# Retention and a gated feed-forward on one core: attention scores as quarter products, and an earlier release of one pair's loads

## The chip, the cores and the metric

The kernel runs on one core of a Trainium2 chip. The core has a matrix engine (TensorE, PE in the profile, with its weight loads as PEld), a vector engine (VectorE, DVE), an activation engine (ScalarE, ACT), GpSimd (POOL), and SyncE (SP), which here issues transfers. Sixteen DMA engines move data. The metric is the device time of one execution in microseconds (us).

## The reference

Retention over four batches and eight heads, 768 steps, 64 elements a head, and then a feed-forward layer with a sigmoid gate on all 3,072 tokens:

```python
gamma = 1 - 2 ** (-5 - arange(H)); scale = 1 / sqrt(D)
for t in range(S):
    state = gamma * state + einsum('bhd,bhe->bhde', k[:, :, t], v[:, :, t])
    y[:, :, t] = scale * einsum('bhd,bhde->bhe', q[:, :, t], state)
x = y.transpose(0, 2, 1, 3).reshape(B * S, H * D)
out = (sigmoid(x @ w_gate) * (x @ w_val)) @ w_out
```

Sizes: x is 3072 x 512, w_gate and w_val 512 x 1536, w_out 1536 x 512. Inputs and output are 32-bit; the kernel multiplies in bf16.

## The kernel before, in words

The 768 steps are cut into six chunks of 128. Two batches of one chunk form a *pair*, so there are 12 pairs, 0 to 11; pair i is chunk i // 2, and within it j = 0, 1 names the batch. The eight heads lie as four columns p of two heads e = 0, 1, and head e occupies partitions 0 to 63 or 64 to 127 (`half(e)`). For the second batch the two heads of a column are swapped.

The work on a pair is written as small functions, each of which issues for its own engines:

- `load_kq`, `load_v` (lines 53 to 72): seven transfers a pair, issued by POOL, which also turn 32-bit into bf16.
- `xbar` (L213): two transposing transfers, issued by SP, k first and then q, into the tile `kqX`. Pair 2 is transposed on TensorE instead (L207).
- `scale_k` (L218): POOL weighs k for the state.
- `inter` (L242): the old state times q, 16 products that use 64 rows and 64 columns of TensorE's array each.
- `scores` (L226): k times q inside the chunk, 16 products of 64 rows and 128 columns, the two heads of a column on the two halves of the rows. They go into four PSUM banks, one for each batch and head.
- `mask` (L232): DVE weighs the scores and writes bf16.
- `intra` (L249): masked scores times v, 16 products of 128 rows and 64 columns, added to what inter left.
- `y_out` (L265): DVE scales the sum into `xT`, the input of the feed-forward.
- `state` (L272), `state_sum` (L281), `casts` (L285): k times v, the running state in 32-bit, and its bf16 copy for a later inter.

`block(old, new)` puts these in TensorE's order: inter of the old pair, scores of the new one, intra of the old one, state of the new one. Either pair may be missing. The steps with both are those of old 4, 5, 6, 7, 8, 9, 10 with new 5 to 11; pairs 3 and 4 have their scores in a step without an old pair, and pair 2 has its own in the middle of the first feed-forward.

The feed-forward runs on a chunk of all four batches, 512 tokens: `up` (L364, L382, L383) for gate and value, `down` (L399, L403) for the output. The order of everything is written out by hand. Pairs 0 and 1 and the first chunk's feed-forward come first; afterwards the list `plan` names, for each chunk, after which group of up or down a step is issued. The tile framework adds the semaphores. Every engine runs its own instructions in the order in which they were issued.

POOL is kept back at seven places by `hold` (L496), a copy of one element of `kqX` into the tile `held`. The copy can start only when the transfer that writes that element has landed, and the load issues behind it on POOL wait with it. The first one stands between `scale_k(3)` and the loads of pairs 4 and 5 (lines 514 to 518). The indices of `kqX` are partition (head and element), k or q, batch, column and token.

PSUM has eight banks, which all parts take in turn from one pool (`pf`, `bank`).

Of the kernel before, what the change touches and what calls it, by code (L numbers as in the profile page):

```python
# [15 lines left out]
def kernel(  # L16
# [12 lines left out]
    nc = tc.nc  # L29
# [3 lines left out]
    C = 128  # L33
    NT = S // C
    NP = H // 2
# [14 lines left out]
    kn, qn, ks, vs, kqT = {}, {}, {}, {}, {}  # L50
# [138 lines left out]
    xT, sc, stA, stB, y, za, zz, zb = {}, {}, {}, {}, {}, {}, {}, {}  # L189

    def bank(shape, dt=F32):
        return pf.tile(shape, dt, tag="ff", name="ff")

    def half(e):
        return slice(e * D, (e + 1) * D)
# [20 lines left out]
    def scale_k(i):  # L216
        ks[i] = ld.tile([C, 2 * H, D], BF16, tag="ks", name="ks", bufs=3)
        nc.gpsimd.tensor_tensor(ks[i], kn[i], tabsk[:, i // 2].rearrange("s j h -> s (j h)").unsqueeze(2)  # L218
                                .to_broadcast([C, 2 * H, D]), op=ALU.mult)

    def scores(i, j):
        t = kqT[i]
        sc[i, j] = (bank([128, NP, C]), bank([128, NP, C]))
        for p in range(NP):
            for e in range(2):
                nc.tensor.matmul(sc[i, j][e][:, p, :], t[half(e), 0, j, p, :], t[half(e), 1, j, p, :],  # L226
                                 start=True, stop=True)

    def mask(i, j, e):
        st = stB if e else stA  # L230
        st[i, j] = at.tile([128, NP, C], BF16, tag=f"st{e}", name=f"st{e}", bufs=4)
        nc.vector.tensor_tensor(st[i, j], sc[i, j][e], maskk[:, e ^ j], op=ALU.mult)  # L232

    def new_y(i):
        for j in range(2):
            y[i, j] = bank([128, NP, C])

    def inter(i):
        for p in range(NP):
            for j in range(2):  # L240
                for e in range(2):
                    nc.tensor.matmul(y[i, j][half(e ^ j), p, :], zb[i - 2][half(e), j, p, :],  # L242
                                     kqT[i][half(e), 1, j, p, :], start=(p == 0), stop=False, skip_group_check=True)

    def intra(i, j):
        for p in range(NP):
            for e in range(2):
                st = (stA, stB)[e ^ j][i, j]
                nc.tensor.matmul(y[i, j][half(e), p, :], vs[i][:, j * H + 2 * p + e, :], st[:, p, :],  # L249
                                 start=False, stop=True, skip_group_check=True)  # L250
# [9 lines left out]
    def y_out(i, j):  # L260
        t = i // 2
        if t not in xT:
            new_xT(t)
        c = (i % 2 * 2 + j) * C
        nc.vector.tensor_tensor(xT[t][0][:, :, c:c + C], y[i, j], taby, op=ALU.mult)  # L265

    def state(i):
        zz[i] = bank([128, 2, NP, D])
        for j in range(2):
            for p in range(NP):  # L270
                for e in range(2):
                    nc.tensor.matmul(zz[i][half(e), j, p, :], ks[i][:, j * H + 2 * p + e, :],  # L272
                                     vs[i][:, j * H + 2 * p + (e ^ j), :],
                                     start=(j == 0 and p == 0), stop=True, skip_group_check=True)
# [4 lines left out]
    def state_sum(i):  # L279
        new_za(i)  # L280
        nc.vector.tensor_tensor(za[i], za[i - 2], zz[i], op=ALU.add)  # L281
# [5 lines left out]
    def block(old, new):  # L287
        last = new is None or new >= NPAIR - 2
        if old is not None:
            new_y(old)  # L290
            inter(old)
        for j in range(2):
            if new is not None:
                scores(new, j)
        for j in range(2):
            if old is not None:
                intra(old, j)
        if not last:
            state(new)
        for j in range(2):  # L300
            if old is not None:
                y_out(old, j)
        for j in range(2):
            if new is not None:
                mask(new, j, 0)
                mask(new, j, 1)
        if not last:
            state_sum(new)
# [180 lines left out]
    def load_next(i):  # L489
        load_kq(i)  # L490
        load_v(i)

    held = const.tile([128, 1], BF16, name="held")

    def hold(i):
        nc.gpsimd.tensor_copy(held, kqT[i][:, 1, 1, NP - 1, C - 1:C])  # L496

    load_next(3)
    scale_k(2)
# [6 lines left out]
    for b in range(3):  # L506
        down(0, b, 6, 9)
    for j in range(2):
        scores(2, j)
        mask(2, j, 0)  # L510
        mask(2, j, 1)
    for b in range(3):
        down(0, b, 9, 12)
    xbar(3)
    scale_k(3)
    hold(3)
    load_next(4)
    load_next(5)
    down(0, 3, 0, 6)
# [4 lines left out]
    for j in range(2):  # L524
# [7 lines left out]

    plan = {
        1: [(2, block, None, 3), (4, block, 3, None), (4, xbar, 4), (4, scale_k, 4), (4, hold, 4), (4, load_next, 6),
            (5, casts, 3), (7, xbar, 5), (7, scale_k, 5), (11, block, None, 4), (12, casts, 4), (12, xbar, 6), (12, scale_k, 6),
            (12, hold, 6), (12, load_next, 7), (14, block, 4, 5), (16, casts, 5), (18, block, 5, 6), (19, casts, 6)],
        2: [(0, xbar, 7), (0, scale_k, 7), (0, hold, 7), (0, load_next, 8), (8, block, 6, 7), (10, casts, 7), (10, xbar, 8),
            (10, scale_k, 8), (10, hold, 8), (10, load_next, 9), (17, block, 7, 8), (19, casts, 8)],
# [47 lines left out]
```

## Time and profile before

| what | value |
|---|---|
| median of 5 runs | 227.84 us (227.26 to 228.27) |
| the profiled execution, its own time | 227.63 us |
| its span, first to last instruction | 225.8 us |
| TensorE busy | 220.4 us (98%) |
| DVE, POOL, ACT busy | 113.4, 106.0, 70.3 us |
| share of the ending chain: up (L364), down (L399) | 54%, 27% |
| the same: scores (L226), inter (L242), intra (L249), state (L272) | 3%, 2%, 3%, 1% |

"Busy" counts an engine's instructions without pauses between them. The chain that ended last is followed back from the last instruction, each time to what released it or to the instruction before it on its engine; its shares say where a saving would reach the end. A line such as L226 is a line of the kernel. Matmul ends are modelled, their starts are recorded, so distances below are taken from start to start.

### The profile page before, as it was taken

The numbers are of one execution on the slowest core, as the hardware profiler recorded it, in microseconds if no ns is written. First come the engines' busy times: TensorE is split into PE (matmuls) and PEld (weight loads), VectorE is DVE, ScalarE is ACT, GpSimd is POOL, SyncE is SP. The second block draws the span as 40 slices with busy tenths as digits, with TensorE's granted clock in tenths as the row PEclk, the third lists the DMA queues.
The fourth block names the chain that finished last, engine by engine and source line by source line (L and its number), as shares of the span: only waits on it lengthen the run. The fifth ranks groups of instructions, "written<-read, shape, count | busy, mean of one in ns | idle before, by whom it ended". The sixth has DMA issues, their size and how long they took to land.

```text
span 225.8 us, 4323 instructions
## 1 busy us (share of the span) xinstructions
PE 220.4 (98%) x1758; PEld 116.9 (52%) x1758; DVE 113.4 (50%) x199; ACT 70.3 (31%) x121; POOL 106.0 (47%) x128
## 2 busy tenths in 40 slices
PE   7899999999999999999999999999999999999994
PEld 2644444558888555445445445445445444444444
DVE  7753653064963996845806535905434802333301
ACT  7584232334233112332222332321432321333221
POOL 8999998845996919359391090730000000000000
PEclk9999999999999999999999999999999999999999
DMA  9999999997999999989999699792600012100022
GB/s 128 153 171 195 191 193 176 168 240 137 116 162 144 154 204 124 140 86 129 85 142 140 139 74 153 56 129 107 139 0 0 3 46 93 49 1 0 0 93 96
DMA packets 105780, 25.72 MB, mean 114 GB/s; under 512 B 94752, under 2 KB 102816, under 8 KB 105760
## 3 DMA queue, kind: packets, MB, share of 16 engines
q0 software_dynamic: 80928, 13.90, 80.2%
q1 hardware_dynamic: 23648, 11.21, 23.5%
q10 hardware_dynamic: 1184, 0.33, 0.6%
q8 instruction: 14, 0.23, 0.4%
q14 instruction: 6, 0.05, 0.1%
HBM read 28.31 MB, written 6.29 MB: 153 GB/s over the span
## 4 chain that ended last, share of the span: by engine, by line
PE 97%; DVE 1%; ACT 1%; issue 0%
PE ff L364 54%; PE ff L399 27%; PE ff L226 3%; PE ff L426 3%; PE ff L249 3%; PE ff L373 2%; PE ff L242 2%; PE ff L412 1%; PE ff L272 1%; ACT kqT L320 1%; PE ff L319 1%; DVE st L326 1%; PE ff L336 0%; PE ff L207 0%; PE ff L350 0%
## 5 line engine op out<-in xcount | busy, mean ns | idle before, releaser
L383 DVE TENSOR_TENSOR hT<-gs,ff 128x512 bf16<-128x512 f32 x72 | 49.0, 686 | 61.2 <-PE ff L364 57.8
L364 PE MATMUL ff<-xT,wg 128*128 128x512 bf16 (+1 forms) x328 | 71.7, 348 | 0.0
L364 PE MATMUL ff<-xT,wv 128*128 128x512 bf16 (+1 forms) x328 | 71.7, 348 | 0.0
L382 ACT ACTIVATE gs<-ff 128x512 f32<-128x512 f32 x72 | 42.9, 597 | 84.1 <-PE ff L364 81.6
L399 PE MATMUL ff<-wo,hT 128*128 128x512 bf16 x276 | 62.1, 379 | 0.0
L364 PEld LDWEIGHTS <-wv 128*128 128x128 bf16 x328 | 32.1, 98 | 28.4
L364 PEld LDWEIGHTS <-wg 128*128 128x128 bf16 x328 | 31.5, 98 | 27.8
L399 PEld LDWEIGHTS <-hT 128*128 128x128 bf16 x276 | 26.3, 98 | 30.7
L403 ACT COPY ob<-ff 128x512 f32<-128x512 f32 x23 | 13.5, 586 | 58.6 <-PE ff L399 58.5
L232 DVE TENSOR_TENSOR st<-ff,maskk 128x512 bf16<-128x512 f32 x40 | 24.7, 680 | 6.4 <-PE ff L226 6.4
L265 DVE TENSOR_TENSOR xT<-ff,taby 128x512 bf16<-128x512 f32 x20 | 12.9, 685 | 28.9 <-PE ff L249 28.9
L496 POOL COPY held<-kqX 128x1 bf16<-128x1 bf16 x7 | 1.8, 259 | 38.0 <-DMA kqX<-qn 38.0
L218 POOL TENSOR_TENSOR ks<-kn,tabsk 128x1024 bf16<-128x1024 bf16 x8 | 15.6, 1959 | 0.4 <-PE ff L399 0.4
L67 POOL DMA_DIRECT2D qn<-in_q_dram x20 | 15.4, 796 | 0.0
L67 POOL DMA_DIRECT2D kn<-in_k_dram x20 | 15.2, 770 | 0.0
L57 POOL DMA_DIRECT2D vs<-in_v_dram x10 | 12.1, 1206 | 1.1 <-DMA wo<-in_moe_w_out_dram 1.0
L285 DVE TENSOR_TENSOR zb<-za,tabz 128x512 bf16<-128x512 f32 x10 | 10.3, 1033 | 0.2
L63 POOL DMA_DIRECT2D kn<-in_k_dram x10 | 9.3, 929 | 1.5 <-issue 1.5
L426 PE MATMUL ff<-zero 128*128 128x512 bf16 x22 | 8.4, 507 | 1.2 <-DVE zero L135 1.2
L63 POOL DMA_DIRECT2D qn<-in_q_dram x10 | 9.2, 921 | 0.0
L249 PE MATMUL ff<-st,vs 128*64 128x128 bf16 x160 | 6.4, 222 | 0.0
L79 POOL DMA_DIRECT2D wg<-in_moe_w_gate_dram x7 | 5.8, 838 | 0.0
(73 smaller groups left out, 118.6 us busy)
## 6 DMA issues: line engine op xcount, KB each, us to landing
out_dram<-ob SPq DMA_DIRECT2D x23, 256.0 KB, 2.6
vs<-in_v_dram POOLq DMA_DIRECT2D x10, 256.0 KB, 6.5
kn<-in_k_dram POOLq DMA_DIRECT2D x13, 128.0 KB, 4.7
qn<-in_q_dram POOLq DMA_DIRECT2D x13, 128.0 KB, 4.6
wo<-in_moe_w_out_dram POOLq DMA_DIRECT2D x4, 384.0 KB, 6.6
wg<-in_moe_w_gate_dram POOLq DMA_DIRECT2D x5, 256.0 KB, 6.1
wv<-in_moe_w_val_dram POOLq DMA_DIRECT2D x5, 256.0 KB, 6.6
kn<-in_k_dram POOLq DMA_DIRECT2D x20, 64.0 KB, 3.6
```

The costliest lines, as they stand in the source:

```text
L63: nc.gpsimd.dma_start(out=tiles[i][:, 0:H], in_=src[0])
L67: nc.gpsimd.dma_start(out=dst[:, e], in_=pairs[:, 1 - e])
L218: nc.gpsimd.tensor_tensor(ks[i], kn[i], tabsk[:, i // 2].rearrange("s j h -> s (j h)").unsqueeze(2) .to_broadcast([C, 2 * H, D]), op=ALU.mult)
L232: nc.vector.tensor_tensor(st[i, j], sc[i, j][e], maskk[:, e ^ j], op=ALU.mult)
L249: nc.tensor.matmul(y[i, j][half(e), p, :], vs[i][:, j * H + 2 * p + e, :], st[:, p, :], start=False, stop=True, skip_group_check=True)
L265: nc.vector.tensor_tensor(xT[t][0][:, :, c:c + C], y[i, j], taby, op=ALU.mult)
L364: nc.tensor.matmul(u[:, i * n:(i + 1) * n], w[:, kk, n1 * 128:(n1 + 1) * 128], x_of(t, kk, lo, hi), start=(kk == 0), stop=(kk == KT - 1))
L382: nc.scalar.activation(g, ps[0], AX.Sigmoid)
L383: nc.vector.tensor_tensor(hT[t][:, n1s[0]:n1s[-1] + 1, lo:hi], g.rearrange("p (i n) -> p i n", n=n), ps[1].rearrange("p (i n) -> p i n", n ...
L399: nc.tensor.matmul(o, hT[t][:, n1, b * C:(b + 1) * C], wo[:, n1, :], start=(n1 == 0), stop=(n1 == NFF - 1))
L403: nc.scalar.copy(ob, o)
L426: nc.tensor.matmul(u, zero[:, :128], zero, start=True, stop=True)
```

## The change

Two things. A new function `quarter_scores` issues the scores as products of 64 rows and 64 columns: each former product is cut in two by the columns of k (g = 0, 1), which gives 32 products a pair, and the output goes to the same banks, half of the partitions at a time. `block` uses it in place of `scores`, and so does pair 2; pairs 0 and 1 keep `scores`. And `hold` takes an argument that chooses k or q; the first hold, that of pair 3, now names k (0), all the others stay at q (1).

```diff
+    def quarter_scores(i, j):
+
+        t = kqT[i]
+        sc[i, j] = (bank([128, NP, C]), bank([128, NP, C]))
+        for p in range(NP):
+            for g in range(2):
+                for e in range(2):
+                    nc.tensor.matmul(sc[i, j][e][half(g), p, :], t[half(e), 0, j, p, half(g)], t[half(e), 1, j, p, :],
+                                     start=True, stop=True)
+
...
         for j in range(2):
             if new is not None:
-                scores(new, j)
+                quarter_scores(new, j)
...
-    def hold(i):
-        nc.gpsimd.tensor_copy(held, kqT[i][:, 1, 1, NP - 1, C - 1:C])
+    def hold(i, which=1):
+        nc.gpsimd.tensor_copy(held, kqT[i][:, which, 1, NP - 1, C - 1:C])
...
     for j in range(2):
-        scores(2, j)
+        quarter_scores(2, j)
         mask(2, j, 0)
         mask(2, j, 1)
...
-    hold(3)
+    hold(3, 0)
     load_next(4)
     load_next(5)
```

## The prediction, made before the result was known

> **What bounds the kernel now.** I read the page first, for the engine that carries the end and for its clock:
>
> ```profile
> span 225.8 us, 4323 instructions
> PE 220.4 (98%) x1758; PEld 116.9 (52%) x1758; DVE 113.4 (50%) x199; ACT 70.3 (31%) x121; POOL 106.0 (47%) x128
> ...
> PEclk9999999999999999999999999999999999999999
> ...
> PE 97%; DVE 1%; ACT 1%; issue 0%
> ```
>
> TensorE is 97% of the chain that ended last, and its granted clock is full in all 40 slices. The list of waits shows no matmul waiting for another engine once the first two pairs are through. So time is saved only by a shorter run of matmuls, and is lost if one has to wait. Next I read TensorE's timeline around the step for old pair 8 and new pair 9, around the first step of pair 3 (scores, then state) and around the last step (pair 11: inter, then intra):
>
> ```profile
> 103.63 0.59 PE L364 MATMUL ff<-xT,wv 128*128 128x512 bf16 x2
> 104.15 0.42 PE L242 MATMUL ff<-kqX,zb 64*64 64x128 bf16 x16
> 104.50 0.62 PE L226 MATMUL ff<-kqX 64*128 64x128 bf16 x16
> 105.05 0.64 PE L249 MATMUL ff<-st,vs 128*64 128x128 bf16 x16
> 105.52 0.42 PE L272 MATMUL ff<-vs,ks 128*64 128x64 bf16 x16
> ```
> ```profile
> 55.80 0.62 PE L226 MATMUL ff<-kqX 64*128 64x128 bf16 x16
> 56.35 0.44 PE L272 MATMUL ff<-vs,ks 128*64 128x64 bf16 x16
> ```
> ```profile
> 187.89 0.42 PE L242 MATMUL ff<-kqX,zb 64*64 64x128 bf16 x16
> 188.23 0.64 PE L249 MATMUL ff<-st,vs 128*64 128x128 bf16 x16
> ```
>
> The first column is the start, the second the length, and "64*128" the part of the array that a matmul uses. The reader is to see how long one kind lasts until the next begins: 0.35 us for inter, 0.55 for scores, 0.47 for intra. A merged row ends with its last matmul, so its length less one matmul gives the spread of its starts. The rows by line give one matmul:
>
> ```profile
> L226 PE MATMUL ff<-kqX x144: 216/216/227, 55.8 to 174.1; 64*128 64x128 bf16 x144
> ```
> ```profile
> L242 PE MATMUL ff<-kqX,zb x144: 216/216/240, 60.3 to 188.1; 64*64 64x128 bf16 x144
> ```
>
> Inter: 0.42 - 0.216 = 0.20 us for 16 starts. In the trace's single starts these are four groups of four, 3 to 4 ns apart inside a group; the second group comes 0.08 after the first, the others every 0.056. Scores: 0.62 - 0.216 = 0.40 us for eight groups of two, the second after 0.066, the others every 0.056. So four quarter products take the time of two half products.
>
> From the start of the last group to the next kind it is 0.15 to 0.16 us wherever the part of the array changes (inter to scores, scores to intra, scores to state, and inter to intra at 188.23). Where it does not change there is no such gap: intra to state, both "128*64", go on after 0.053 (105.05 + 0.64 - 0.219 = 105.47, and state starts at 105.52). A change of shape thus costs about 0.10 us more than an ordinary group.
>
> **The change, part by part.**
>
> Scores as quarters. Per pair, 16 half products go and 32 quarter products come, in eight groups of four instead of eight groups of two. The running rate is not shown for 32 quarters in a row; nearest are the 16 of inter, 0.056 per group, the same interval as now. Upper bound: only two of four run at once (scores' own pairs: two per 0.056), then +0.45 us per pair. Lower bound: state's two-wide groups, which stream half as many columns, start every 0.028; but the present groups of 128 columns all take 0.053 to 0.056, so I exclude a gain. I take 0.056, as inter has this very shape, these four places and two banks for the two row halves.
>
> Inter to scores. In seven steps (new pairs 5 to 11) scores follow inter directly. Bounds: 0.056, as if one kind went on (0.053 at intra to state), or 0.15 as today. I take 0.056, since the shape is then the same. From inter's start to intra's start now: 105.05 - 104.15 = 0.90. Then: twelve groups, 0.08 + 10 x 0.056 = 0.64, and the way out to intra 0.156 as for pair 11 (188.23 - 187.89 - 0.19), together 0.796. That is -0.104 each, -0.73 for seven.
>
> Pairs 2, 3 and 4 follow full-array matmuls. Entry 0.31 before and after (inter after such a matmul has it: 103.63 + 0.59 - 0.379 = 103.84 to 104.15), first group 0.08 in place of 0.066, exit 0.156 in place of 0.149: 0.08 + 6 x 0.056 + 0.156 = 0.57 instead of 0.55. +0.02 each, +0.06 for three.
>
> Weight loads: 32 instead of 16 per pair, 106 ns instead of 94 each, beside matmuls (inter's are hidden today). Uncovered, 8 x 12 ns = 0.1 us a pair.
>
> The masks read the same four banks, a tenth of a microsecond earlier in the seven steps. DVE moves with TensorE there: at 105.51 it had been idle for 0.49 us, so output and masks shift along.
>
> The earlier release on POOL. The copy that holds POOL waits for the crossbar of pair 3's k instead of q. Views of the issues and of the copy:
>
> ```profile
> L213 SPq DMA_TRANSPOSE kqX<-kn x1: 1492/1492/1492, 47.9 to 47.9; - x1
> L213 SPq DMA_TRANSPOSE kqX<-qn x1: 1850/1850/1850, 49.5 to 49.5; - x1
> ```
> ```profile
> 53.50:54.00 0.50, 0.50 (x7) 0.45 (x6) 0.00 (x0) 0.39 (x1) 0.44 (x2) 1.00 0.13 45
> 54.00:54.50 0.50, 0.50 (x7) 0.45 (x5) 0.27 (x1) 0.00 (x0) 0.50 (x1) 1.00 0.00 0
> 54.50:55.00 0.50, 0.50 (x7) 0.45 (x5) 0.42 (x1) 0.00 (x0) 0.50 (x2) 1.00 0.00 0
> ```
>
> By its time to landing k lands at 47.88 + 4.74 = 52.62, q at 49.49 + 3.95 = 53.43 (the copy started at 53.49). So the 14 transfer issues of pairs 4 and 5 behind it on POOL, the scaling of k for pair 4 (65.5 us), and on SP the crossbars of pair 4, which wait for those loads, come up to 0.81 us earlier. The windows (last two columns DMA share and GB/s) show nothing moving from 54.0 to 55.0 after the first issue at 53.73: packets come 1.5 us behind it. Released at 52.7 they would start near 54.4, and q has landed a microsecond before. So q of pair 3, needed at 55.80, keeps its 2.4 us. Worth on the path: 0, because pair 4's q lands at 69.26 (62.41 + 6.86) for scores at 73.64 and pair 5's at 76.70 for scores at 78.84. Bounds: a gain is excluded, no matmul waits for either; if the loads did catch q, the longest landing of the crossbar (7.3 us) puts it at 56.8, a stall of 1.0 us.
>
> Sum: -0.73 + 0.06 + 0 = -0.67 us. The profiled execution took 227.63 us (span 225.8 and 1.8 around it), so 226.96; the median of the runs is 0.21 above it, so **227.17**, or -0.29%.
>
> **A cost that the trace only bounds: feeding TensorE.** Inter, scores, intra and state make 64 pairs of load and matmul today, 80 then. Two sequencer rows show how quickly pairs are handed over:
>
> ```profile
> L226 PEldq EVENT_SEMAPHORE  x1: 51/51/51, 104.2 to 104.2; - x1
> ```
> ```profile
> L272 PEldq EVENT_SEMAPHORE  x1: 51/51/51, 105.1 to 105.1; - x1
> ```
>
> The first stands ahead of scores, the second ahead of state. Between them 16 scores and 16 intra pairs, 64 instructions, were handed over in 0.9 - 0.05 = 0.85 us: at most 13.3 ns each, 26.6 a pair. The quarters use 14 a pair (0.056 / 4). Both events come about 20 ns after the start of the kind before them (104.15, 105.05), and so does state's event of pair 3 (55.8, scores start 55.80), where the sequencer had 2 us. So it was waiting for room, not behind. I take it as fast enough; the bound goes to the rivals.
>
> The Trainium skill, Runtime: NRT & Kernel Launch, section "Instruction fetch mechanics", names a floor of about 20 sequencer cycles for an instruction; TensorE: Matmul & The Clock Gate, section "Wait — 56ns, not 53.3ns?", gives that sequencer 1.2 GHz. An estimate from the two pages is 33 ns a pair, which would put seven steps late by 0.4 to 0.7 us each and the run near 232. The 64 instructions in 0.85 us are already quicker than that floor, so the measurement decides.
>
> **Rivals.**
> 1. The sequencer limits (slower). Place: the 32 quarters after inter, handed over from 104.25 on. At 26.6 ns a pair the last starts at 105.10 instead of 104.79; state's last, 64 pairs and one event later, at 106.0, today 105.75. +0.25 in five steps with state, +0.2 in two without: +1.65 + 0.06, so 229.5. It cancels the gain from about 22 ns a pair on. For it: no stretch of 48 quarters exists today. Against: the 20 ns above.
> 2. The shape still changes, or is charged anyway, between inter and scores: ten times +0.02, 228.0. Against: intra to state.
> 3. Two wide only: 10 x 0.45, near 232.
> 4. A late crossbar, or POOL's earlier scaling blocking DVE at a worse moment: up to +1.0, 228.2. Against: the spare times above.
> 5. A better way out of the quarters, or a wait unseen by me removed: 226.8.
>
> **How the numbers follow.** As computed 64%, 226.9 to 227.5 by the spread of the runs (227.26 to 228.27 before); rival 1 13%, rival 2 8%, rivals 3 and 4 4% each, rival 5 7%. A measurement of this kernel tells about 0.3%, 0.68 us, from no change: the limit is 227.16, in the middle of the computed case, which I split 35 to 29. Faster 0.35 + 0.07 = 0.42; same 0.29 + 0.08 + 0.03 (a mild rival 1) = 0.40; slower 0.10 + 0.04 + 0.04 = 0.18. The range 226.7 to 228.2 holds the computed case and rivals 2, 4 and 5, and leaves out most of rivals 1 and 3.
>
> **What would show it.** Right: 32 scores matmuls "64*64" in a pair; scores' first start 0.25 after inter's first instead of 0.35; inter to intra 0.80 instead of 0.90; pairs 3 and 4 at 0.57; POOL's first copy near 52.7; no matmul waiting. Wrong: groups of four more than 0.056 apart, above all late among the 32 (rival 1); 0.35 still there (rival 2); scores of pair 3 waiting for q (rival 4).

## The result, and the profile after

The changed kernel takes 226.81 us in the median of 27 runs (226.52 to 227.91); the kernel before took 227.75 us in the median of 51 (227.2 to 229.41). The ratio is 0.9958, with a 95% interval of 0.9947 to 0.9969: faster by 0.94 us in the medians, 0.42%. The forecast was 227.17 us, -0.67 us, in a range of 226.7 to 228.2.

The page of the changed kernel:

```profile
span 224.7 us, 4643 instructions
PE 219.4 (98%) x1918; PEld 116.2 (52%) x1918; DVE 113.1 (50%) x199; ACT 70.4 (31%) x121; POOL 105.5 (47%) x128
```

There are 160 more matmuls, and TensorE's busy time and the span are both smaller. Its timeline around the same three steps (start, length, engine, line, operation; scores are L236 now, inter L252, intra L259, state L282):

```profile
103.68 0.42 PE L252 MATMUL ff<-kqX,zb 64*64 64x128 bf16 x16
103.92 0.62 PE L236 MATMUL ff<-kqX 64*64 64x128 bf16 x32
104.47 0.64 PE L259 MATMUL ff<-st,vs 128*64 128x128 bf16 x16
104.94 0.42 PE L282 MATMUL ff<-vs,ks 128*64 128x64 bf16 x16
```
```profile
55.50 0.64 PE L236 MATMUL ff<-kqX 64*64 64x128 bf16 x32
56.07 0.44 PE L282 MATMUL ff<-vs,ks 128*64 128x64 bf16 x16
```
```profile
186.88 0.42 PE L252 MATMUL ff<-kqX,zb 64*64 64x128 bf16 x16
187.23 0.64 PE L259 MATMUL ff<-st,vs 128*64 128x128 bf16 x16
```

Scores now begin 0.24 us after inter (0.35 before), inter to intra is 0.79 us (0.90 before, 0.796 forecast), and a pair's scores without an inter ahead take 0.57 us (0.55 before, 0.57 forecast). Pair 11, where nothing was changed, still has 0.35. From the first matmul of the first feed-forward, which starts at 15.29 us (15.61 before), to the first down after pair 11's intra, at 187.80 (188.80 before), it is 172.51 us against 173.19: -0.68, the sum of the forecast to 0.01 us. The rest of the difference between the two spans (225.8 and 224.7) is the earlier start, -0.32, which varies from execution to execution (15.29 to 15.62 us in the profiles of this study), and some 0.05 at the end. Two further profiles of the changed kernel show 172.60 and 172.72 us for the same stretch; in both the difference stands at 18.8 us, where the first feed-forward waited 0.09 and 0.21 us for weights.

The copy that holds POOL, and the crossbar transfers of pair 3 (durations in ns, and behind the comma the first and the last start in us):

```profile
L506 POOL COPY held<-kqX x1: 191/191/191, 52.9 to 52.9; 128x1 bf16<-128x1 bf16 x1
```
```profile
L213 SPq DMA_TRANSPOSE kqX<-kn x1: 2062/2062/2062, 47.6 to 47.6; - x1
L213 SPq DMA_TRANSPOSE kqX<-qn x1: 1947/1947/1947, 49.8 to 49.8; - x1
```

The copy runs at 52.9 instead of 53.49, though the transfers themselves landed a little later here (k at 52.86, q at 53.76). In these two profiles no matmul waits for anything after the first pairs, so they show no use for the release. The medians, however, moved 0.27 us more than the sum, and the upper end of the runs came down: 18 of the 51 runs before were above 228.0, 0.8 us over the lowest, and 5 of the 27 after are as far above theirs. That was the question for the experiments.

### The profile page after: what moved, and what is told of

It is laid out like the page before. It is cut to its first block, busy times and chain, and to the rows that moved or that the text cites. A ratio compares the mean times of both kernels' runs of the same rounds, so it can differ in the third digit from the quotient of the medians.

```text
span 224.7 us, 4643 instructions
## 1 busy us (share of the span) xinstructions
PE 219.4 (98%) x1918; PEld 116.2 (52%) x1918; DVE 113.1 (50%) x199; ACT 70.4 (31%) x121; POOL 105.5 (47%) x128
## 4 chain that ended last, share of the span: by engine, by line
PE 93%; POOL 2%; DMA 2%; issue 0%; DVE 0%; POOLq 0%
PE ff L374 54%; PE ff L409 27%; PE ff L259 3%; DMA vs<-in_v_dram 2%; PE ff L236 2%; PE ff L383 2%; PE ff L252 2%; POOL kn L92 1%; PE ff L422 1%; POOL qn L92 1%; PE ff L282 1%; PE ff L436 1%; PE ff L346 1%; PE ff L207 0%; PE ff L360 0%
## 5 line engine op out<-in xcount | busy, mean ns | idle before, releaser
L506 POOL COPY held<-kqX 128x1 bf16<-128x1 bf16 x7 | 1.3, 186 | 39.3 <-DMA kqX<-qn 34.5
L259 PE MATMUL ff<-st,vs 128*64 128x128 bf16 x160 | 6.4, 222 | 0.0
L336 DVE TENSOR_TENSOR st<-ff,decay 128x512 bf16<-128x512 f32 x8 | 5.2, 686 | 1.5 <-PE ff L226 0.9
```

## The experiments

Two theories stood against each other: A, the shape change between inter and scores is the whole gain and the release is worth nothing; B, the release gave a part. Medians are compared with the kernel before in the same group of runs, on the same chip; the ratios are formed over all the runs of a group and need not equal the quotient of the medians.

**The two parts, one at a time.** The quarters alone, run twice:

```diff
-    hold(3, 0)
+    hold(3)
```

> The changed kernel with its first hold back at pair 3's q, so the quarter products alone. Theory A (the whole gain is the shape change that is gone between inter and scores in seven steps, -0.73, less 0.06 for the slower entry of pairs 2, 3 and 4; the release is worth nothing): median 0.67 below the kernel before, ratio 0.997, and the same as the changed kernel within 0.1 us. Theory B (the runs of the changed kernel moved by 0.94 us in their median, 0.27 more than that sum, and the earlier release gave the rest): ratio 0.997 too, but the changed kernel run beside it is 0.27 us quicker than this one. In the profile both expect 0.25 us from inter's first start to scores' first start and first loads of pair 4 about 0.8 us later than in the changed kernel.

> The quarter products alone once more, beside the changed kernel. Theory A (the release is worth nothing; the 0.65 us between the two medians, 227.30 and 226.65, was scatter): both medians equal within 0.15 us. Theory B2 (without the release some executions have pair 5's scores wait for the crossbar of its q, as in the profile of the one-batch run, where it landed at 78.72 us): this one 0.3 to 0.6 us above the changed kernel, with most of its runs between 226.6 and 227.7.

The release alone, run twice, is the changed kernel with `scores` put back at both places:

```diff
-                quarter_scores(new, j)
+                scores(new, j)
...
-        quarter_scores(2, j)
+        scores(2, j)
```

> Scores as half products everywhere, as before, and only the first hold moved to pair 3's k. Theory A: no matmul waits for these loads, so ratio 1.000 (within 0.1 us of the kernel before). Theory B: 0.27 us below the kernel before, ratio 0.9988. Both expect the copy on POOL near 52.7 to 53 us instead of 53.5, and inter to scores still 0.35 us.

> Half products as before and only the first hold moved to pair 3's k, once more. Theory B2 (the release spares waits of some executions around pair 5: scores for its q, state for its scaled k, down for a bank that the output of pair 4 frees late): 0.1 to 0.5 us below the kernel before in the median, depending on how many of that kernel's runs wait, with fewer runs above 228. Theory D (the release matters only together with the quarters): equal to the kernel before within 0.1.

And the changed kernel itself, beside the first and the second of the quarters alone:

> The changed kernel again, beside the others on one chip. Theory A: 0.67 below the kernel before (0.9971), equal to the quarters alone. Theory B: 0.94 below (0.9958), which is the sum of the two parts.

> The changed kernel once more. Both theories: 226.5 to 226.9, ratio 0.995 to 0.997. Its pair 5 q should land near 77.2 us, a microsecond ahead of the scores that read it at 78.5.

| kernel | median us | before, same group | ratio, 95% interval |
|---|---|---|---|
| quarters alone, first | 227.30 | 227.55 | 0.998 (0.9961 to 0.9999) |
| release alone, first | 227.71 | 227.55 | 1.0003 (0.9982 to 1.0024) |
| changed kernel, with the first | 226.65 | 227.55 | 0.995 (0.9931 to 0.997) |
| quarters alone, second | 227.96 | 228.05 | 0.9992 (0.9972 to 1.0012) |
| changed kernel, with the second | 226.84 | 228.05 | 0.9947 (0.9927 to 0.9968) |
| release alone, second | 227.65 | 227.89 | 0.9982 (0.9963 to 1.0002) |

Theory A fails for the release: with the quarters in place it is worth 0.65 us in the first group (227.30 to 226.65) and 1.12 in the second (227.96 to 226.84). The runs of the quarters alone go from 226.58 to 228.87, and in the second group half of them lie above 228, as do half of the runs of the kernel before (12 of 24); of the 13 runs of the changed kernel beside them none is above 227.24. Theory A holds for the rest: the profile of the quarters alone has the same steps as the changed kernel,

```profile
104.02 0.42 PE L252 MATMUL ff<-kqX,zb 64*64 64x128 bf16 x16
104.27 0.62 PE L236 MATMUL ff<-kqX 64*64 64x128 bf16 x32
104.81 0.58 PE L259 MATMUL ff<-st,vs 128*64 128x128 bf16 x14
```

so its 0.7 us are there, and in many runs something takes them back. A little of that is in the two profiles themselves, both of quick runs (226.83 and 227.13 us). In the first, state of pair 5 starts 0.66 us after intra instead of 0.47, because it waits for POOL's scaled k:

```profile
79.15 0.64 PE L259 MATMUL ff<-st,vs 128*64 128x128 bf16 x16
79.81 0.44 PE L282 MATMUL ff<-vs,ks 128*64 128x64 bf16 x16
```

In the second, down waits 0.31 us at 81.8 for an output of pair 4. From the first feed-forward to the first down after pair 11 they take 172.72 and 172.82 us; without these waits that is 172.53 and 172.51, as in the changed kernel. In neither do pair 5's scores wait for q. The release alone is unclear in both groups: +0.16 and -0.24 in the medians, with intervals that contain 1.

**Half of the scores as quarters.** From the kernel before, with `quarter_scores` added:

```diff
-                scores(new, j)
+                (quarter_scores if j == 0 and old is not None else scores)(new, j)
```

> In the seven steps that have an inter, only the first batch's scores are quarter products and the second batch's stay half products; pairs 2 to 4 and the hold are as before. The shape then still changes once between inter and intra's shape, only one batch later. Theory A: no gain, inter's start to intra's start 0.90 us as before, ratio 1.000; the gap of 0.15 us stands between the two batches. Theory C (quarter products are quicker in themselves, whatever stands before them): half of the gain, inter to intra 0.85, -0.36 us, ratio 0.9984.

Median 227.51 against 227.55, ratio 0.9997 (0.9982 to 1.0013). Its timeline:

```profile
104.29 0.42 PE L252 MATMUL ff<-kqX,zb 64*64 64x128 bf16 x16
104.54 0.39 PE L236 MATMUL ff<-kqX 64*64 64x128 bf16 x16
104.87 0.40 PE L226 MATMUL ff<-kqX 64*128 64x128 bf16 x8
105.19 0.64 PE L259 MATMUL ff<-st,vs 128*64 128x128 bf16 x16
```

Inter to intra is 0.90 us as before: the quarters follow inter after 0.25 us, and the 0.1 us is paid a little later, between the quarters and the half products (0.33 for four groups that need 0.22). Quarter products are not quicker in themselves; what they save is the change of shape. Theory C falls.

The same profile also held the first direct sight of the other effect. The chain that ended last, around pair 5's scores (start, us, what):

```profile
49.45 4.83 DMA kqX<-qn
54.33 0.19 POOL held L506
...
64.47 6.83 DMA qn<-in_q_dram
71.44 7.28 DMA kqX<-qn
78.72 0.14 issue
78.85 0.42 PE ff L236 x16
```

In this execution q of pair 3 landed at 54.3 instead of 53.4, the loads behind the hold came a microsecond later, pair 5's q was loaded at 71.3, and its crossbar landed at 78.72. Inter of pair 4 had started at 78.24, its scores could have followed at 78.49 and waited 0.37 us. In the profile before, the same transfer had landed at 76.70 with 2.1 us to spare.

**The suspected wait made larger.** The quarters alone, with two operations on POOL behind the first hold:

```diff
     hold(3)
+    late = const.tile([128, NP, C], F32, name="late")
+    for _ in range(2):
+        nc.gpsimd.tensor_tensor(late, causal.unsqueeze(1).to_broadcast([128, NP, C]),
+                                tabsk[:, 0, 0, 0::2].unsqueeze(2).to_broadcast([128, NP, C]), op=ALU.mult)
```

> The quarter products alone, with two more operations of about 1.07 us each on POOL behind the first hold (they write a tile that nobody reads), so that the loads of pairs 4 and 5 start some 2.1 us later. Theory A, with the spare 2.1 us between landing and use of the profile before: no more than 0.1 to 0.2 us above the quarters alone. Theory B2, with a spare between 0 and 3 us from execution to execution: pair 5's scores wait in most runs, 0.7 to 2 us above the quarters alone, and the gap stands between inter of pair 4 and scores of pair 5.

Median 231.0 against 228.05 of the kernel before, ratio 1.0124 (1.0092 to 1.0155): 3.0 us above the quarters alone of the same group, more than the delay put in. The timeline (in brackets the idle time ahead and what ended it):

```profile
78.42 0.42 PE L252 MATMUL ff<-kqX,zb 64*64 64x128 bf16 x16
82.00 0.64 PE L236 MATMUL ff<-kqX 64*64 64x128 bf16 x32 [3.17 <-DMA kqX<-qn]
82.57 0.64 PE L259 MATMUL ff<-st,vs 128*64 128x128 bf16 x16
83.05 0.42 PE L282 MATMUL ff<-vs,ks 128*64 128x64 bf16 x16
83.79 6.64 PE L409 MATMUL ff<-wo,hT 128*128 128x512 bf16 x23 [0.33 <-issue]
```

Pair 5's scores waited 3.3 us for its q, and from state to the next inter (at 90.36) it took 7.3 us instead of 5.6 in the changed kernel (79.49 to 85.12). What lengthened the second stretch is the granted clock of TensorE, the third column from the end in these windows:

```profile
83.00:84.00 1.00, 0.67 (x25) 0.62 (x21) 0.97 (x2) 0.00 (x0) 0.00 (x0) 0.72 2.02 166
84.00:85.00 1.00, 1.00 (x3) 0.29 (x2) 1.00 (x3) 0.00 (x0) 0.00 (x0) 0.50 1.28 237
85.00:86.00 1.00, 1.00 (x4) 0.37 (x3) 1.00 (x2) 0.00 (x0) 0.00 (x0) 0.50 1.26 328
86.00:87.00 1.00, 1.00 (x4) 0.36 (x3) 1.00 (x3) 0.59 (x1) 0.36 (x2) 0.57 0.39 150
```

After 3.2 us without a matmul the clock stood at about half for more than 3 us; the four windows lack 1.7 us of clock in all, which is the 7.3 against 5.6. So the wait was paid for once and a half. Five of the six runs have a mean clock of 0.992 or 0.993 in this kernel, and the sixth, at 0.999, is the quickest (230.02). A wait of 1.4 us in another profile below left the clock at 1.00. Theory A's spare of 2.1 us does not hold in this kernel, where loads that were issued 2.4 us later than in the quarters alone left q 3.2 us late, and what stands behind the first hold reaches the path.

**The hold taken away.**

```diff
-    hold(3, 0)
     load_next(4)
     load_next(5)
```

> The changed kernel without its first hold: the loads of pairs 4 and 5 are issued about 5 us earlier, near 48, beside the crossbars of pair 3. Theory A: pair 4's and 5's crossbars land earlier for nothing; if the loads slow pair 3's crossbars past 55.4 us, where its scores start, the run is longer by the overshoot (landing at most 9.5 us after its issue at 49.7: up to 3.8 us). Theory B2: pair 5's q lands several microseconds ahead of 78.5, so no wait there, and the median is at or under the changed kernel's unless pair 3 is late in the same way.

Median 228.34 against 228.05, ratio 1.0019 (0.9995 to 1.0044), and 1.5 us above the changed kernel. Pair 3's scores come 6.33 us after the up before them began, 5.33 in the changed kernel, and start at 57.00:

```profile
55.04 1.04 PE L374 MATMUL ff<-xT,wv 128*128 128x256 bf16 x8
57.00 0.64 PE L236 MATMUL ff<-kqX 64*64 64x128 bf16 x32 [0.93 <-DVE hT L393]
```
```profile
L213 SPq DMA_TRANSPOSE kqX<-qn x1: 1870/1870/1870, 50.4 to 50.4; - x1
...
DMA to landing us min/median/max: 6.5/6.5/6.6
```

The bracket names DVE, which had been done for long; q was issued at 50.41 and took 6.45 us to land, at 56.86, against 4.0 us in the changed kernel, and scores started 0.14 us behind it. So loads beside pair 3's crossbars do slow them, by 2.4 us here, and cost a wait of 1.0 us. This is the fourth rival of the prediction, in a kernel that provokes it. The release to k stays on the good side: nothing moves between 54.0 and 54.5 in the changed kernel's windows, and q had landed at 53.76, before the first of the new loads' packets.

**Which wait is it?** In the profile of the second release alone, the slowest of its twelve runs, it was another one. DVE there:

```profile
77.56 3.89 DVE L295 TENSOR_TENSOR zb<-za,tabz 128x512 bf16<-128x512 f32 x1
81.37 1.27 DVE L275 TENSOR_TENSOR xT<-ff,taby 128x512 bf16<-128x512 f32 x2
```
```profile
77.05 3.84 POOL L218 TENSOR_TENSOR ks<-kn,tabsk 128x1024 bf16<-128x1024 bf16 x2
```
```profile
80.31 1.47 PE L409 MATMUL ff<-wo,hT 128*128 128x512 bf16 x6
82.10 2.10 PE L409 MATMUL ff<-wo,hT 128*128 128x512 bf16 x9 [0.33 <-DVE xT L275]
```

The bf16 copy of pair 4's state, 0.69 us long where POOL is quiet, lasted 3.89 us and ended 0.56 us after POOL's two scalings of k. The Trainium skill, SBUF — State Buffer, section "SBUF: two separate sides", has DVE and GpSimd share a pair of ports that one holds for a whole instruction while the other blocks, where the DVE operation has two inputs in SBUF and GpSimd's reads SBUF too; that is so here, and the copy that outlasts both scalings agrees with it. Pair 4's output stood behind the copy, and down waited 0.5 us for the output. POOL's scalings come behind its loads, so a later release moves this wait as well. To see whether it is the main one, the quarters alone with that copy issued behind the step of pairs 4 and 5:

```diff
-(12, casts, 4), (12, xbar, 6)
+(12, xbar, 6)
...
-(14, block, 4, 5), (16, casts, 5)
+(14, block, 4, 5), (15, casts, 4), (16, casts, 5)
```

> The quarter products alone, first hold at q, with the bf16 copy of pair 4's state issued behind the step of pairs 4 and 5. If what the release spares is mainly the wait of down behind that copy (DVE holds it while POOL scales k, 3.62 us in the profile of the quarters alone, and the output of pair 4 starts only at 81.1), the median comes down to that of the changed kernel, 226.7 to 226.9, ratio 0.995 to 0.997. If it is mainly pair 5's scores waiting for q, nothing is gained: ratio 0.998 to 0.999 as for the quarters alone.

Median 227.96 against 227.89, ratio 1.0005 (0.9979 to 1.0032): nothing gained. Its profile has no long copy any more, but

```profile
78.43 0.42 PE L252 MATMUL ff<-kqX,zb 64*64 64x128 bf16 x16
80.22 0.64 PE L236 MATMUL ff<-kqX 64*64 64x128 bf16 x32 [1.37 <-DMA kqX<-qn]
```

pair 5's scores waited 1.5 us for q, which landed at 80.08. So the copy behind POOL is not what the release mainly spares; the crossbar of pair 5's q is the likelier one. That it is the main wait of the quarters alone is not shown: of its runs only two quick ones have a profile, and there q came in time.

The kept profiles show why q comes close at all. The third column is the time from the first load of pair 4 behind the hold to the landing of pair 5's last load of q, the fourth how far ahead of its scores the crossbar of that q landed (us, one figure for each profile):

| kernel | first hold | first load to q loaded | spare of the crossbar |
|---|---|---|---|
| before | q | 16.1 | 2.1 |
| release alone | k | 16.3, 17.3 | 3.1, 2.4 |
| one batch as quarters (pairs 2 to 4 half products) | q | 16.7 | -0.2 |
| quarters alone | q | 18.9, 18.5 | 0.3, 1.1 |
| quarters with the late copy | q | 19.1 | -1.4 |
| changed kernel | k | 18.5, 18.4, 19.2 | 1.2, 1.5, 0.9 |

Wherever pairs 2 to 4 have quarter products, these loads take about 2 us longer (18.3 and 18.4 in the kernels with later loads and with smaller products, 16.5 in the version below, which goes back to half products there), and most of the spare time of the kernel before is gone; the release gives 0.8 us back. With one batch as quarters the loads are quick, but they began 0.8 us late, and the crossbar itself took 7.3 us. Why the loads take longer is not shown. One thing that differs in the traces is a 16 KB transfer of instructions: it starts at 68.7 to 70.2 us in the lower three kernels, while the loads are in flight, and at 71.2 to 72.1 us in the upper three, behind them. No run tests whether it matters.

**A version made from this.** The changed kernel with half products again for pairs 2, 3 and 4, and the late copy:

```diff
-                quarter_scores(new, j)
+                (scores if old is None else quarter_scores)(new, j)
...
-        quarter_scores(2, j)
+        scores(2, j)
...
-(12, casts, 4), (12, xbar, 6)
+(12, xbar, 6)
...
-(14, block, 4, 5), (16, casts, 5)
+(14, block, 4, 5), (15, casts, 4), (16, casts, 5)
```

> The changed kernel with half products again for pairs 2, 3 and 4, and with the bf16 copy of pair 4's state issued three groups later, behind the step of pairs 4 and 5, so that the output of pair 4 does not stand behind it on DVE. Expected: pairs 2 to 4 back at 0.55 us for their scores, 0.06 us less in all; output of pair 4 on DVE near 79.9 instead of 80.5; median 0.05 to 0.1 below the changed kernel, 226.5 to 226.7, ratio 0.994 to 0.996.

226.92 against 227.89, ratio 0.9961 (0.9936 to 0.9986), which is not told apart from the changed kernel and not the 0.05 to 0.1 us below it that were expected. Pairs 2 to 4 are back at 0.55 us. Seven of its twelve runs are under 227.0; the profiled one, 227.61, has no wait around pair 5 but lost 0.9 us between 18 and 20 us, where the first feed-forward waited for its weights.

**Smaller products still.** Each quarter product cut into two of 64 moving columns:

```diff
+            for m in range(2):
...
-                    nc.tensor.matmul(sc[i, j][e][half(g), p, :], t[half(e), 0, j, p, half(g)], t[half(e), 1, j, p, :],
-                                     start=True, stop=True)
+                        nc.tensor.matmul(sc[i, j][e][half(g), p, half(m)], t[half(e), 0, j, p, half(g)],
+                                         t[half(e), 1, j, p, half(m)], start=True, stop=True)
```

> The changed kernel with each quarter product cut once more, into two of 64 moving columns: 64 scores products a pair, the same array work. Theory of a sequencer with room to spare: state's groups of 64 columns start every 28 ns, so 16 groups of four take 0.45 us as now, inter to intra 0.80, the same time. Theory of a limit on handing over (at most 26.6 ns a pair of load and matmul was shown, 14 in the quarters): a group of four then lasts longer than 28 ns; at 14 ns a pair scores take 0.90 instead of 0.45, +4.5 us over ten pairs.

```profile
105.22 0.42 PE L253 MATMUL ff<-kqX,zb 64*64 64x128 bf16 x16
105.46 0.71 PE L237 MATMUL ff<-kqX 64*64 64x64 bf16 x64
106.11 0.64 PE L260 MATMUL ff<-st,vs 128*64 128x128 bf16 x16
```

Median 228.29 against 227.89, ratio 1.0011 (0.9987 to 1.0034). Scores to intra is 0.65 us instead of 0.55, so ten pairs cost 1.0 us more, and inter to intra is 0.89, nearly as with the half products. The single starts of the 64 products have two parts: the first half comes in groups of four, 32 ns apart, and from then on one product starts every 8.3 ns without groups. Pair 3's, which follow a long stretch of full-array products, keep to groups of four almost to the end. A group of four every 32 ns is 8.0 ns a product, so the rate itself hardly changes.

## Why the prediction was right, and where it was not

**Scores as quarters, 0.056 us per group:** right. 32 quarters run in eight groups of four at 0.056, as inter's 16 do; the upper bound of two at a time did not occur.

**Inter to scores at 0.056 instead of 0.15:** right. The step is 0.79 us, 0.796 forecast; the kernel with one batch as quarters shows that the 0.10 us belong to the change of shape, since they come back where the shape changes one batch later.

**Pairs 2, 3 and 4, +0.02 each:** right, 0.57 us.

**Weight loads hidden:** right. The row of single loads gives 103 to 107 ns, and no group is longer for it.

**The release, "Worth on the path: 0", with the words "a gain is excluded":** this is the step that failed. The spare times of 4.4 us for pair 4 and 2.1 us for pair 5 were read from one execution of the kernel before and taken to hold for the changed kernel. With the quarters and the same hold, the spare of pair 5's q is 0.3 and 1.1 us in two profiles of quick runs and less than nothing in the one with the late copy. The chain is hold, loads of pairs 4 and 5, crossbar of pair 5's q, scores of pair 5, and beside it POOL's scaling of k with the waits behind that; 0.8 us earlier at its head is worth 0.65 and 1.12 us in the medians with the quarters in place. It is by this term that the measured -0.94 exceeds the -0.67. The forecast still came within 0.4 us because the term is small, and for that it gave no reason. And without it the other term would hardly have shown: the quarters alone came to -0.25 and -0.09.

**No collision of the earlier loads with q:** right for this release; without the hold q is slowed from 4.0 to 6.45 us and pair 3 waits 1.0 us.

**The feeding of TensorE, bound at 26.6 ns a pair of load and matmul, 14 needed, taken as fast enough:** right, and with room to spare. With 64 products the starts settle at 8.3 ns each, so handing over takes no more than that. The 33 ns estimated from the Trainium skill (Runtime: NRT & Kernel Launch, "Instruction fetch mechanics") is four times too slow here; its floor for an instruction does not bind weight loads and matmuls in these runs.

What stays open. The table of spare times fits what the parts do: the release alone has nothing to shorten where q is 2 to 3 us early, the quarters alone use that time up, and both together leave 0.9 to 1.5 us. But it rests on one execution of each run, so how many runs wait, and where, was not counted. The medians of the parts add up to -0.1 (first group) and about -0.3 (second groups) against 0.9 to 1.2 us for both together, their runs spread over 2 us, and the intervals of the release alone contain no change. And the kernel before has slow runs too, 18 of 51 above 228.0 us, though its one profile has 2.1 us to spare; what they wait for no profile shows.

## What to carry to other kernels

Look for neighbouring groups of matmuls that use different parts of TensorE's array: each change cost 0.10 us here, and writing one group in the shape of the other removed it, although that took twice the instructions. And do not carry a transfer's spare time from the trace of the kernel before over to the changed one: 2.1 us there was 0.3 and 1.1 us with the quarters and the same hold, and less than nothing in two related kernels, because loads and crossbar took longer. Such a chain of hold, load and crossbar belongs into the sum, or at least into the range, even when nothing waits for it in the profile at hand.

## What was not expected of the hardware

Handing over a pair of weight load and matmul takes at most 8.3 ns: with 64 products of 64 columns in a row, the starts go from groups of four every 32 ns to single starts every 8.3 ns once the stock in the queue is used up. That the sequencer sets this figure is read from the pattern and was not tested by itself; as groups of four come at 8.0 ns a product, the array's own rate may set it as well.

A gap in the matmuls can cost more than its length: after 3.2 us without one the granted clock stood at about half for more than 3 us, worth another 1.7 us.

The time that a crossbar transfer takes to land varies widely, and with the loads beside it: pair 3's q took 3.3 to 5.0 us with the hold in place and 6.45 without it, and pair 4's q up to 11.1 us, issued at 61.66 among the loads of pair 5 in the quarters with the late copy.
